# A diffusion-transformer block on one core: two modulation vectors computed ahead of V, a K tile split earlier, two LN2 chunks on another engine

## The chip, the cores and the metric

The kernel runs on one core of a Trainium2 chip. The metric is the device time of one execution in microseconds (us). The kernel before takes 244.02 us, the median of three runs (243.87 to 244.14). The profiled execution, whose trace is read below, took 243.82 us by the same clock; the trace itself spans 242.1 us from the first instruction to the last. All positions in this document are microseconds from the start of that span.

A core has five engines, each with a queue of its own: PE (TensorE, matmuls; PEld is its weight load), DVE (VectorE), ACT (ScalarE), POOL (GpSimd) and SP (SyncE, which issues most of the transfers here). [...]

## The reference

The block has two batch elements of 256 tokens, width D = 1152, two heads, and an MLP of width 4608. Everything that goes in and out is bfloat16. Cut to what matters:

```python
mod = (_silu(c) @ w_mod).reshape(B, 6, 1, D)
shift_a, scale_a, gate_a, shift_m, scale_m, gate_m = [mod[:, i] for i in range(6)]
h = _layernorm(x, axis=-1) * (1 + scale_a) + shift_a
qkv = (h @ wqkv).reshape(B, N, 3, H, Dh)
q, k, v = (qkv[:, :, 0].copy(), qkv[:, :, 1].copy(), qkv[:, :, 2].copy())
attn = _softmax(jnp.einsum('bqhd,bkhd->bhqk', q, k) * Dh ** (-0.5), axis=-1)
a = jnp.einsum('bhqk,bkhd->bqhd', attn, v).reshape(B, N, D) @ wo
x = x + gate_a * a
h2 = _layernorm(x, axis=-1) * (1 + scale_m) + shift_m
m = _gelu(h2 @ w_fc1) @ w_fc2
return x + gate_m * m
```

## The kernel before

Activations lie transposed, feature chunk by feature chunk: D is KD = 9 chunks of P = 128. The four token tiles (t = 0..3) are two for each batch element b. Weights go through a pool of five large buffers of 128 x 9 x 1152 elements, and a tile of the pool gets its place when it is first written.

**K and the shift.** K is computed from h without the shift: a constant added to all keys moves all scores of a row alike, and softmax drops it. Q and V need the shift. So K's tiles 0 to 5 run step by step as chunks arrive (`k_step`), its tiles 6, 7 and 8 run as whole panels, and inside the last panel the shift vector is computed, so that DVE and ACT can add it to h while PE finishes the panel.

```python
    for g, (k0, k1) in enumerate(KGROUPS):            # [(0, 2), (2, 4), (4, 6), (6, 9)]
        load_scale_group(g, nc.sync)
        for k in range(k0, k1):
            nc.sync.dma_start(w_k[:, k, 0:KM1 * P], wqkv_v[:, k, D:D + KM1 * P])       # KM1 = 6
    nc.sync.dma_start(w_k[:, :, KM1 * P:D], wqkv_v[:, :, D + KM1 * P:2 * D])
    # ... cut ...
    k_panel(6)
    k_evac(6)
    k_panel(7)
    k_evac(7)
    k_panel(8, 0, 5)                                  # chunks 0..4 of the last panel
    shift_a = vec_section(sT, w_shift_a, "shift_a")   # 36 narrow matmuls, then a DVE transpose
    k_panel(8, 5)                                     # chunks 5..8
    hT = act.tile([P, KD, T], BF16, name="hT")
    for k in range(KD):
        for b in range(B):
            dst, src = hT[:, k, b * N:(b + 1) * N], hT0[:, k, b * N:(b + 1) * N]
            if (k * B + b) % 3 < 2:
                nc.vector.tensor_scalar_add(dst, src, shift_a[:, k, b:b + 1])
            else:
                nc.scalar.activation(dst, src, ACT.Identity, bias=shift_a[:, k, b:b + 1])
        if k == 2:
            k_evac(8)
```

`vec_section` and `gate_natural` put the two rows of silu(c) on the array as a stationary operand of 32 columns and stream the weight past it, four column strips at a time. Q follows: six tiles together over the nine chunks (54 matmuls, line 511), then three tiles one by one (27, line 519), then the scores.

**The modulation vectors of the second half.** The gate of the attention branch (36 matmuls) goes through DRAM and comes back broadcast to all partitions. Two thirds of the MLP's scale are dot products on DVE against transposed weights (`scale_m_dots`); the last third (`scale_mN`) is 36 narrow matmuls. Both groups of matmuls stand after the second V group:

```python
    load_scale_mT(0)                                  # transposing load
    load_v(0)
    load_section("w_gate_a", S_GATE_A, w_gate_a)      # three pieces
    nc.sync.dma_start(w_scale_mN, wmod_v[:, :, S_SCALE_M * D + NDOT * P:(S_SCALE_M + 1) * D])
    load_v(1)
    load_scale_mT(CPP)
    load_v(2)
    # ... Q, the scores: cut ...
    for i, (pnl, t) in enumerate(v_order):            # 3 panels x 4 token tiles
        # softmax pieces and the transposes of the attention before the first three groups: cut
        v_group(pnl, t)                               # 9 matmuls 128x384, ACT copies the result
        if i == 1:
            gate_a = gate_natural(0, w_gate_a)
            scale_mN = vec_section(sT, w_scale_mN, "scale_mN", KD - NDOT)
        if i == 2:
            scale_m_dots(CPP, NDOT)
            # ... add one: cut ...
```

**LN2 and the start of FC1.** After the output projection (`wo_group(t, i)`), each token tile is normalized and transposed by a transfer into `hT`; `ln2_modulate` applies scale and shift in place. The nine chunks of batch 0 are modulated while PE still works on the output projection of tile 3; FC1 begins with batch 0 and takes the chunks in the order 0 to 8.

```python
    def ln2_modulate(b, ks=range(KD)):
        for k in ks:
            h = hT[:, k, b * N:(b + 1) * N]
            if b == 0 and k == KD - 1:
                nc.gpsimd.tensor_scalar(h, h, scale_m[:, k, b:b + 1], shift_m[:, k, b:b + 1], ...)
            elif b == 0 or k % 3 == 2:
                nc.scalar.activation(h, h, ACT.Identity, bias=shift_m[:, k, b:b + 1], scale=scale_m[:, k, b:b + 1])
            else:
                nc.vector.tensor_scalar(h, h, scale_m[:, k, b:b + 1], shift_m[:, k, b:b + 1], ...)
    # ...
    wo_group(3, 0)
    ln2_modulate(0, range(6))
    ln2_stats(2, 2)
    ln2_sqrt(2)
    ln2_modulate(0, range(6, KD))
    wo_group(3, 1)
    ln2_stats(3, 0)
    ln2_recip(2)
    ln2_normalize(2)
    ln2_transpose(2)
    wo_group(3, 2)
    wo_group(3, 3)
```

FC1 (432 matmuls, line 802) and FC2 (468, line 866) take the rest.

Of the kernel before, what the change touches and what calls it, by code (L numbers as in the profile page):

```python
# [19 lines left out]
def kernel(  # L20
# [11 lines left out]
    nc = tc.nc  # L32
    B, N, D = x.shape
# [3 lines left out]
    P = 128  # L37
# [3 lines left out]
    KD = D // P  # L41
# [17 lines left out]
    def acc_tile(shape, name, dt=FP32):  # L59
        return psum.tile(shape, dt, name=name, tag="acc", bufs=6)  # L60

    def aux_tile(shape, name, dt=FP32):
        return psum.tile(shape, dt, name=name, tag="aux", bufs=2)
# [5 lines left out]
    wqkv_v = wqkv.rearrange("(k p) n -> p k n", p=P)  # L69
# [7 lines left out]
    def wide_tile(name):  # L77
        return wide.tile([P, KD, D], BF16, name=name, tag="wide")
# [19 lines left out]

    KGROUPS = [(0, 2), (2, 4), (4, 6), (6, 9)]
    KM1 = 6  # L100
    w_scale_a = wide_tile("w_scale_a")
    w_k = wide_tile("w_k")

    def load_scale_group(g, eng):
        c0, c1 = KGROUPS[g][0] * P, KGROUPS[g][1] * P
        eng.dma_start(w_scale_a[:, :, c0:c1], wmod_v[:, :, S_SCALE_A * D + c0:S_SCALE_A * D + c1])

    for g, (k0, k1) in enumerate(KGROUPS):
        load_scale_group(g, nc.sync)
        for k in range(k0, k1):  # L110
            nc.sync.dma_start(w_k[:, k, 0:KM1 * P], wqkv_v[:, k, D:D + KM1 * P])
    nc.sync.dma_start(w_k[:, :, KM1 * P:D], wqkv_v[:, :, D + KM1 * P:2 * D])

    def load_section(name, s, w=None):
        w = wide_tile(name) if w is None else w
        for r in range(0, KD, 3):
            nc.sync.dma_start(w[:, r:r + 3, :], wmod_v[:, r:r + 3, s * D:(s + 1) * D])
        return w
# [9 lines left out]
    for r in range(0, KD, 3):  # L128
        nc.sync.dma_start(w_q[:, r:r + 3, 0:KM1 * P], wqkv_v[:, r:r + 3, 0:KM1 * P])
    nc.sync.dma_start(w_q[:, :, KM1 * P:D], wqkv_v[:, :, KM1 * P:D])  # L130
    w_scale_m = wide_tile("w_scale_m")
# [8 lines left out]
    def load_scale_mT(j):  # L140
        c0 = S_SCALE_M * D + j * P
        nc.sync.dma_start_transpose(w_scale_mT[:, j:j + CPP, :], w_mod[:, c0:c0 + PW])

    def load_o(n):
        nc.sync.dma_start(w_o[:, :, n * PW:(n + 1) * PW], wo_v[:, :, n * PW:(n + 1) * PW])
# [5 lines left out]
    def load_v(n):  # L151
        nc.sync.dma_start(w_v[:, :, n * PW:(n + 1) * PW], wqkv_v[:, :, 2 * D + n * PW:2 * D + (n + 1) * PW])
# [75 lines left out]
    def norm1(t, c0, c1, eng):  # L228
        if eng == "a":
            nc.scalar.activation(  # L230
                xns[t][:, c0:c1], x_sb[:, t, c0:c1], ACT.Identity,
                bias=nb1[:, t:t + 1], scale=rstd1[:, t:t + 1],
            )
        else:
            nc.vector.tensor_scalar(
                xns[t][:, c0:c1], x_sb[:, t, c0:c1], mv1[:, t, 0:1], rstd1[:, t:t + 1],
                op0=ALU.subtract, op1=ALU.mult,
            )
# [30 lines left out]
    def modulate(pt, i, k, t0, j0, w, eng):  # L269
        b = t0 // TPB  # L270
        dst, src, sc = hT0[:, k, t0 * P:t0 * P + w], pt[:, i, j0:j0 + w], scale_a[:, k, b:b + 1]
        if eng == "d":
            nc.vector.tensor_scalar_mul(dst, src, sc)
        else:
            nc.scalar.mul(dst, src, sc)
# [7 lines left out]

    def k_step(k, c0=0, c1=T, m0=0, m1=KM1):
        for m in range(m0, m1):
            if k == 0 and c0 == 0:
                pk[m] = acc_tile([P, T], "pk")
            nc.tensor.matmul(  # L288
                pk[m][:, c0:c1], w_k[:, k, m * P:(m + 1) * P], hT0[:, k, c0:c1],
                start=(k == 0 and c0 == 0), stop=(k == KD - 1), skip_group_check=True,  # L290
            )
# [19 lines left out]
    def k_evac(m):  # L311
        evac(kT[:, m, :], pk[m][:])

    def k_panel(m, ka=0, kb=KD):
        if ka == 0:
            pk[m] = acc_tile([P, T], "pk")
        for k in range(ka, kb):
            nc.tensor.matmul(  # L318
                pk[m][:], w_k[:, k, m * P:(m + 1) * P], hT0[:, k, :],
                start=(k == 0), stop=(k == KD - 1),  # L320
            )
# [70 lines left out]
    for k in range(2):  # L392
        modulate(pt_4, k, k, 3, 0, P, "d")
    k_step(3, 0, N, 3, KM1)
    norm1(1, CUT, D, "d")
# [31 lines left out]
    def vec_section(stat, w, name, nk=KD):  # L427
        pn = aux_tile([P, nk * 32], "pn")
        for k in range(KD):
            wk4 = w[:, k, :].rearrange("p (j q r) -> p q j r", q=4, r=32)  # L430
            for i in range(4):
                nc.tensor.matmul(  # L432
                    pn[32 * i:32 * i + SW, :].rearrange("p (j r) -> p j r", r=32),
                    stat[:, k, :], wk4[:, i, :, :],
                    start=(k == 0), stop=(k == KD - 1), tile_position=(0, 32 * i),
                )
        dst = act.tile([P, nk, 32], FP32, name=name)
        nc.vector.transpose(dst[:].rearrange("p k c -> p (k c)"), pn[:])
        return dst
# [2 lines left out]
    k_evac(6)  # L442
    k_panel(7)
    k_evac(7)
    k_panel(8, 0, 5)
    shift_a = vec_section(sT, w_shift_a, "shift_a")
    k_panel(8, 5)

    hT = act.tile([P, KD, T], BF16, name="hT")
    for k in range(KD):  # L450
        for b in range(B):
            dst, src = hT[:, k, b * N:(b + 1) * N], hT0[:, k, b * N:(b + 1) * N]
            if (k * B + b) % 3 < 2:
                nc.vector.tensor_scalar_add(dst, src, shift_a[:, k, b:b + 1])
            else:
                nc.scalar.activation(dst, src, ACT.Identity, bias=shift_a[:, k, b:b + 1])
        if k == 2:
            k_evac(8)
# [32 lines left out]
    for b in range(B):  # L491
        nc.sync.dma_start(s_b[b][:], s_dram[b:b + 1, :].partition_broadcast(P))
    load_scale_mT(0)
    load_v(0)
    load_section("w_gate_a", S_GATE_A, w_gate_a)
    nc.sync.dma_start(w_scale_mN, wmod_v[:, :, S_SCALE_M * D + NDOT * P:(S_SCALE_M + 1) * D])
    load_v(1)
    load_scale_mT(CPP)
    load_v(2)
# [81 lines left out]
    def v_group(pnl, t):  # L581
        pacc = acc_tile([P, PW], "pacc")
        for k in range(KD):
            nc.tensor.matmul(  # L584
                pacc[:], hT[:, k, t * P:(t + 1) * P], w_v[:, k, pnl * PW:(pnl + 1) * PW],
                start=(k == 0), stop=(k == KD - 1),
            )
        nc.scalar.copy(v_sb[:, t, pnl * PW:(pnl + 1) * PW], pacc[:])
# [3 lines left out]
    for i, (pnl, t) in enumerate(v_order):  # L592
        for j in ((0, 1), (2,), (3,))[i] if i < 3 else ():
            softmax(j // H, j % H)
            if j % H == H - 1:
                attn_transpose(j // H)
                for n in ((0,), (1, 2))[j // H]:
                    load_o(n)
        v_group(pnl, t)
        if i == 1:  # L600
            gate_a = gate_natural(0, w_gate_a)
            scale_mN = vec_section(sT, w_scale_mN, "scale_mN", KD - NDOT)
        if i == 2:
            scale_m_dots(CPP, NDOT)
            nc.vector.tensor_scalar_add(scale_m[:, 0:NDOT, :], scale_m[:, 0:NDOT, :], 1.0)
            nc.vector.tensor_scalar_add(scale_m[:, NDOT:KD, :], scale_mN[:, :, 0:B], 1.0)
# [52 lines left out]
    def ln2_recip(t):  # L659
        nc.vector.reciprocal(rstds[t][:], rstds[t][:])  # L660
        nbs[t] = small.tile([P, 1], FP32, name="nb", tag="nb")
        nc.vector.tensor_scalar(nbs[t][:], mv2[:, t, 0:1], rstds[t][:], -1.0, op0=ALU.mult, op1=ALU.mult)
# [16 lines left out]
# [4 lines that stand above are left out]
                nc.gpsimd.tensor_scalar(  # L683
                    h, h, scale_m[:, k, b:b + 1], shift_m[:, k, b:b + 1], op0=ALU.mult, op1=ALU.add,
                )
            elif b == 0 or k % 3 == 2:
                nc.scalar.activation(  # L687
                    h, h, ACT.Identity, bias=shift_m[:, k, b:b + 1], scale=scale_m[:, k, b:b + 1],
                )
            else:  # L690
                nc.vector.tensor_scalar(
                    h, h, scale_m[:, k, b:b + 1], shift_m[:, k, b:b + 1], op0=ALU.mult, op1=ALU.add,
                )
# [21 lines left out]
    def ln2_stats(t, i):  # L715
        c0, c1 = cuts[t][i:i + 2]
        nc.vector.bn_stats(stats2[t][:, i, :], x1[:, t, c0:c1])
# [33 lines left out]
    ln2_modulate(0, range(6))  # L751
    ln2_stats(2, 2)
    ln2_sqrt(2)
    ln2_modulate(0, range(6, KD))
    wo_group(3, 1)
    ln2_stats(3, 0)
    ln2_recip(2)
    ln2_normalize(2)
    ln2_transpose(2)
# [100 lines left out]
    for gi, (n, t, c0, cw) in enumerate(groups):  # L860
        b = t // TPB
# [59 lines left out]
```

## Time and profile before

| what | value |
|---|---|
| median of 3 runs | 244.02 us |
| span of the trace | 242.1 us |
| PE busy | 235.3 us, 1698 matmuls |
| DVE, ACT, POOL busy | 93.4, 69.5, 32.0 us |
| bytes moved | 54.48 MB, mean 225 GB/s |
| FC2, FC1 matmuls (lines 866, 802) | 70.5 us, 70.5 us |
| V matmuls (line 584) | 17.9 us |

The profile counts an engine busy from an instruction's start to its modelled end. Matmuls overlap, so a matmul listed with 379 ns can follow the one before it after 216 ns: the rate at which PE works is read from the starts, not from the durations. Four views matter here. The timeline of an engine lists its instructions in order of time, merged where they are alike, with start, length and count. The list of waits tells who waited for whom. The chain of waits goes back from the last instruction to what released it, step by step. The lines on transfers give the size and the time from issue to landing.

### The profile page before, as it was taken

The page shows a single profiled execution, that of the slowest core. Times are in us where ns is not written, and L with a number is a line of the kernel's source. Part 1 is how long each engine was busy: PE and PEld are TensorE (multiplying, and loading weights), DVE is VectorE, ACT ScalarE, POOL GpSimd, SP SyncE. Part 2 cuts the span into 40 slices and gives each one's busy share as a digit, 9 for nine tenths or more (in the row PEclk, how much of TensorE's full clock was granted, in tenths as well). Part 3 has the DMA queues.
Part 4 walks back from the last instruction along what each step waited for, and adds up shares of the span by engine and source line. Part 5 has one row for each costly group of instructions (what it writes and reads, how often), then busy time and mean ns, then how long its engine had stood idle before and what let it go on. Part 6 is the DMA issues. An engine that isn't in the chain of part 4 may idle for free.

```text
span 242.1 us, 4031 instructions
## 1 busy us (share of the span) xinstructions
PE 235.3 (97%) x1698; PEld 142.7 (59%) x1698; DVE 93.4 (39%) x209; ACT 69.5 (29%) x138; POOL 32.0 (13%) x48
## 2 busy tenths in 40 slices
PE   8799999999999999999999999999999999999994
PEld 2486444466656666888844444444566656665573
DVE  2872550675694676720000019999002000000001
ACT  6532250543735174782222233322000000000000
POOL 1000400000310616300000000000314111111111
PEclk9999999999999999999999999999999999999999
DMA  6999999999999999799999999996891000000000
GB/s 223 324 330 360 379 344 247 326 372 284 254 322 361 380 255 208 208 219 327 327 328 249 191 274 328 327 326 188 245 286 39 19 16 16 20 20 27 19 19 16
DMA packets 76989, 54.48 MB, mean 225 GB/s; under 512 B 26011, under 2 KB 72491, under 8 KB 76971
## 3 DMA queue, kind: packets, MB, share of 16 engines
q1 hardware_dynamic: 76240, 53.02, 77.7%
q0 software_dynamic: 704, 1.20, 1.6%
q8 instruction: 13, 0.21, 0.4%
q14 instruction: 5, 0.04, 0.0%
q10 hardware_dynamic: 27, 0.00, 0.0%
HBM read 46.90 MB, written 1.19 MB: 199 GB/s over the span
## 4 chain that ended last, share of the span: by engine, by line
PE 91%; DMA 3%; ACT 2%; DVE 2%; issue 0%; SPq 0%; DVEq 0%
PE pacc L866 29%; PE pacc L802 29%; PE pacc L584 7%; PE pacc L705 6%; PE pacc L511 5%; PE pk L288 4%; DMA w_scale_a<-in_w_mod_dram 3%; PE pacc L519 2%; PE pk L318 2%; ACT hT L687 2%; PE pa L619 1%; PE ps_s L539 1%; PE pn L432 1%; PE pm L248 1%; PE pt L266 1%; PE pg L467 1%
## 5 line engine op out<-in xcount | busy, mean ns | idle before, releaser
L802 PE MATMUL pacc<-hT,w_f 128*128 128x256 bf16 (+1 forms) x432 | 70.5, 326 | 0.2 <-ACT hT L687 0.2
L866 PE MATMUL pacc<-w_f,gT 128*128 128x384 bf16 (+2 forms) x468 | 70.5, 314 | 0.0
L866 PEld LDWEIGHTS <-gT 128*128 128x128 bf16 x468 | 44.4, 98 | 26.2
L802 PEld LDWEIGHTS <-w_f 128*128 128x128 bf16 x432 | 42.2, 98 | 28.0 <-issue 0.4
L485 DVE SCALAR_TENSOR_TENSOR late<-w_gate_mT,late 128x1152 bf16<-128x1152 bf16 x18 | 24.4, 1358 | 36.8 <-DMA w_gate_mT<-in_w_mod_dram 36.2
L872 DVE TENSOR_TENSOR tmp<-pacc,gate 128x384 f32<-128x384 f32 (+2 forms) x13 | 6.8, 527 | 62.5 <-PE pacc L866 50.5
L840 ACT ACTIVATE gT<-pacc 128x512 bf16<-128x512 f32 x24 | 14.3, 597 | 32.3 <-PE pacc L802 32.3
L485 DVE SCALAR_TENSOR_TENSOR s_spill<-w_scale_m,s_b 128x1152 bf16<-128x1152 bf16 x12 | 16.3, 1357 | 8.5 <-DMA w_scale_m<-in_w_mod_dram 8.2
L705 PE MATMUL pacc<-w_o,big 128*128 128x384 bf16 (+2 forms) x117 | 17.9, 314 | 0.0
L874 POOL TENSOR_TENSOR o_sb<-tmp,x 128x384 bf16<-128x384 f32 (+1 forms) x12 | 11.7, 974 | 47.4 <-DVE tmp L872 47.4
L584 PE MATMUL pacc<-w_v,hT 128*128 128x384 bf16 x108 | 17.9, 326 | 0.0
L705 PEld LDWEIGHTS <-big 128*128 128x128 bf16 x117 | 11.0, 98 | 6.8 <-ACT big L627 0.2
L584 PEld LDWEIGHTS <-hT 128*128 128x128 bf16 x108 | 10.4, 98 | 7.0 <-issue 0.2
L288 PE MATMUL pk<-big,w_k 128*128 128x128 bf16 (+2 forms) x102 | 13.3, 278 | 0.0
L711 POOL TENSOR_TENSOR x<-tmp,x_sb 128x384 f32<-128x384 f32 (+1 forms) x11 | 9.8, 891 | 17.4 <-DVE tmp L710 9.5
L511 PE MATMUL pacc<-hT,w_q 128*128 128x512 bf16 x54 | 11.8, 379 | 0.1
L327 POOL DMA_DIRECT2D gates_dram<-grow x4 | 2.1, 521 | 70.8 <-DVE grow L826 70.8
L818 ACT ACTIVATE gT<-pacc 128x512 bf16<-128x512 f32 x12 | 6.9, 597 | 10.4 <-PE pacc L802 10.4
L288 PEld LDWEIGHTS <-w_k 128*128 128x128 bf16 x102 | 7.8, 98 | 3.0
L511 PEld LDWEIGHTS <-w_q 128*128 128x128 bf16 x54 | 5.3, 98 | 6.7 <-issue 0.4
L710 DVE TENSOR_TENSOR tmp<-pacc,gate 128x384 f32<-128x384 f32 (+2 forms) x13 | 6.7, 522 | 5.4 <-PE pacc L705 5.2
L523 ACT ACTIVATE big<-pacc 128x512 bf16<-128x512 f32 x9 | 4.8, 608 | 11.5 <-PE pacc L511 8.8
(101 smaller groups left out, 160.9 us busy)
## 6 DMA issues: line engine op xcount, KB each, us to landing
w_f<-in_w_fc_dram SPq DMA_DIRECT2D x14, 864.0 KB, 11.0
w_f<-in_w_fc_dram SPq DMA_DIRECT2D x2, 2592.0 KB, 10.7
w_f<-in_w_fc_dram SPq DMA_DIRECT2D x2, 1728.0 KB, 13.8
w_shift_a<-in_w_mod_dram SPq DMA_DIRECT2D x3, 864.0 KB, 10.5
w_v<-in_wqkv_dram SPq DMA_DIRECT2D x3, 864.0 KB, 6.0
w_gate_a<-in_w_mod_dram SPq DMA_DIRECT2D x3, 864.0 KB, 9.2
w_o<-in_wo_dram SPq DMA_DIRECT2D x3, 864.0 KB, 6.2
w_shift_m<-in_w_mod_dram SPq DMA_DIRECT2D x3, 864.0 KB, 13.0
```

Source lines behind the costliest of these rows:

```text
L288: nc.tensor.matmul(pk[m][:, c0:c1], w_k[:, k, m * P:(m + 1) * P], hT0[:, k, c0:c1], start=(k == 0 and c0 == 0), stop=(k == KD - 1), skip_g ...
L485: nc.vector.scalar_tensor_tensor(spill, wT[:, j, :], 1.0, s_b[b], op0=ALU.mult, op1=ALU.mult, accum_out=dst(j, b),)
L511: nc.tensor.matmul(pq[m][:], w_q[:, k, m * P:(m + 1) * P], hT[:, k, :], start=(k == 0), stop=(k == KD - 1),)
L584: nc.tensor.matmul(pacc[:], hT[:, k, t * P:(t + 1) * P], w_v[:, k, pnl * PW:(pnl + 1) * PW], start=(k == 0), stop=(k == KD - 1),)
L705: nc.tensor.matmul(pacc[:], aT[:, k, t * P:(t + 1) * P], w_o[:, k, c0:c1], start=(k == ks[0]), stop=(k == ks[-1]),)
L711: (nc.vector if (t, i) in ((1, 2), (3, 3)) else nc.gpsimd).tensor_tensor(x1[:, t, c0:c1], tmp[:], x_sb[:, t, c0:c1], op=ALU.add)
L802: nc.tensor.matmul(dst, w_f1[m // KD][:, k, ml * P:(ml + 1) * P], hT[:, k, c0:c1], start=(k == 0), stop=(k == KD - 1),)
L818: nc.scalar.activation(gT[:, ms[0]:ms[-1] + 1, b * N:(b + 1) * N], pacc[:], ACT.Gelu_apprx_tanh)
L840: nc.scalar.activation(gT[:, m, :], pacc[:], ACT.Gelu_apprx_tanh)
L866: nc.tensor.matmul(pacc[:], gT[:, kk, t * P:(t + 1) * P], w_f2[j][:, r, c0 - n * PW:c0 - n * PW + cw], start=(kk == 0), stop=(kk == KF - 1),)
L872: nc.vector.tensor_tensor(tmp[:], pacc[:], gate_m[:, b, c0:c0 + cw], op=ALU.mult)
L874: (nc.vector if last else nc.gpsimd).tensor_tensor(o_sb[:], tmp[:], x1[:, t, c0:c0 + cw], op=ALU.add)
```

## The change

The change has three parts, all of them moves: the same values are computed with the same number of matmuls.

First, the attention gate and the last third of the MLP's scale are computed before the first V group instead of after the second, and their loads are issued ahead of the first V load. The first V group then begins with its matmuls after them.

Second, the last K panel is cut after 3 of its 9 chunks instead of after 5, so that the shift vector is computed sooner and six matmuls instead of four run while it is transposed and added. The adds are dealt differently: batch 0 and the odd chunks on DVE, the even chunks of batch 1 on ACT (13 and 5, before 12 and 6). The K weight's rows 6 to 8 are loaded whole, and the late load of columns 768 to 1151 shrinks to rows 0 to 5.

Third, two of the nine LN2 chunks of batch 0 (6 and 7) move from ACT to DVE, where they stand behind the first statistics of tile 3; the last chunk stays on POOL.

```diff
-            nc.sync.dma_start(w_k[:, k, 0:KM1 * P], wqkv_v[:, k, D:D + KM1 * P])
-    nc.sync.dma_start(w_k[:, :, KM1 * P:D], wqkv_v[:, :, D + KM1 * P:2 * D])
+            c1 = KM1 * P if k < KWHOLE else D          # KWHOLE = 6
+            nc.sync.dma_start(w_k[:, k, 0:c1], wqkv_v[:, k, D:D + c1])
+    nc.sync.dma_start(w_k[:, 0:KWHOLE, KM1 * P:D], wqkv_v[:, 0:KWHOLE, D + KM1 * P:2 * D])
...
-    k_panel(8, 0, 5)
+    k_panel(8, 0, 3)
     shift_a = vec_section(sT, w_shift_a, "shift_a")
-    k_panel(8, 5)
+    k_panel(8, 3)
...
-            if (k * B + b) % 3 < 2:
+            if b == 0 or k % 2:
                 nc.vector.tensor_scalar_add(dst, src, shift_a[:, k, b:b + 1])
...
     load_scale_mT(0)
-    load_v(0)
     load_section("w_gate_a", S_GATE_A, w_gate_a)
     nc.sync.dma_start(w_scale_mN, wmod_v[:, :, S_SCALE_M * D + NDOT * P:(S_SCALE_M + 1) * D])
+    load_v(0)
     load_v(1)
...
-        v_group(pnl, t)
-        if i == 1:
+        if i == 0:
             gate_a = gate_natural(0, w_gate_a)
             scale_mN = vec_section(sT, w_scale_mN, "scale_mN", KD - NDOT)
+        v_group(pnl, t)
...
-            elif b == 0 or k % 3 == 2:
+            elif k < 6 if b == 0 else k % 3 == 2:
                 nc.scalar.activation(
...
-    ln2_modulate(0, range(6, KD))
+    ln2_modulate(0, [KD - 1])
     wo_group(3, 1)
     ln2_stats(3, 0)
+    ln2_modulate(0, range(6, KD - 1))
     ln2_recip(2)
```

More of the change, by code (lines that the diff above doesn't have):

```diff
@@ L100 @@
     KM1 = 6
+    KWHOLE = 6
     w_scale_a = wide_tile("w_scale_a")
```

## The prediction

> **What bounds the kernel now.** I read the page's busy times first, then PE's waits, then PE's timeline at the three places that the change touches, and last the landings of the loads around V.
>
> ```profile
> PE 235.3 (97%) x1698; PEld 142.7 (59%) x1698; DVE 93.4 (39%) x209; ACT 69.5 (29%) x138; POOL 32.0 (13%) x48
> ...
> PE   8799999999999999999999999999999999999994
> ```
>
> PE is full from the second slice of 6 us to the last but one. The other engines and the transfers matter only where they make PE wait. The list of PE's waits has just one entry after the start-up:
>
> ```profile
> PE pacc L802 <- ACT hT L687: 0.2, 1, 0.2
> ```
>
> So no large gain is to be had: 2% would be 4.9 us, and the list has not 1 us of waits in the body. But the durations are modelled longer than the spacing, so a short gap can hide between a modelled end and the next start. I look for gaps in the starts.
>
> PE's timeline around the shift vector:
>
> ```profile
> 26.26 5.13 PE L318 MATMUL pk<-big,w_k 128*128 128x512 bf16 x23
> 31.32 1.29 PE L432 MATMUL pn<-w_shift_a,sT 128*32 128x288 bf16 x36
> 32.54 1.04 PE L318 MATMUL pk<-big,w_k 128*128 128x512 bf16 x4
> 33.72 2.53 PE L511 MATMUL pacc<-hT,w_q 128*128 128x512 bf16 x11
> ```
>
> A 128x512 matmul takes 0.216 us from start to start (27 of them take 5.83 us in line 519 of the chain of waits). Four from 32.54 use PE's time up to 33.41, but Q starts at 33.72: a gap of 0.31 us. VectorE and ScalarE at that time:
>
> ```profile
> 32.66 0.48 DVE L438 STREAM_TRANSPOSE shift_a<-pn 128x288 f32<-128x288 f32 x1 [3.56 <-PE pn L432]
> 33.18 0.87 DVE L454 TENSOR_SCALAR hT<-big,shift_a 128x256 bf16<-128x256 bf16 x4
> ```
>
> The first chunk needs two of these adds, both on DVE: the second starts 0.2 us after the first and takes 0.28, so the chunk is ready at 33.66, which is Q's start less a semaphore's delay.
>
> PE's timeline around V:
>
> ```profile
> 54.78 0.61 PE L548 MATMUL ps_s<-big 64*128 64x256 bf16 x8
> 55.33 3.10 PE L584 MATMUL pacc<-w_v,hT 128*128 128x384 bf16 x18
> 58.35 1.29 PE L467 MATMUL pg<-w_gate_a,sT 128*32 128x288 bf16 x36
> 59.47 0.56 PE L432 MATMUL pn<-w_scale_m,sT 128*32 128x96 bf16 x36
> 59.95 2.29 PE L584 MATMUL pacc<-w_v,hT 128*128 128x384 bf16 x13
> ```
>
> From 55.33 to 59.95 PE goes without a wait. The step is 0.163 us per V matmul (90 in 14.73 us in the chain of waits).
>
> PE's timeline at the start of FC1:
>
> ```profile
> 97.64 0.93 PE L802 MATMUL pacc<-hT,w_f 128*128 128x256 bf16 x7
> 98.75 2.45 PE L802 MATMUL pacc<-hT,w_f 128*128 128x256 bf16 x21 [0.18 <-ACT hT L687]
> ```
>
> Seven matmuls at 0.109 us (16 of 128x256 take 1.75 us in line 619 of the chain) reach to 98.40; the eighth, which needs chunk 7, starts at 98.75. The gap is 0.35 us and not the 0.18 counted. ACT's timeline tells why:
>
> ```profile
> 94.48 3.06 ACT L687 ACTIVATE hT<-hT,shift_m,scale_m 128x256 bf16<-128x256 bf16 x6 [3.60 <-DVE stats L717]
> 97.44 0.28 ACT L657 ACTIVATE rstd<-mv,eps_t 128x1 f32<-128x1 f32 x1
> 97.62 1.08 ACT L687 ACTIVATE hT<-hT,shift_m,scale_m 128x256 bf16<-128x256 bf16 x2
> ```
>
> Six chunks, a square root, then chunks 6 and 7, the last ready at 98.70.
>
> The loads around V, as SyncE issues them:
>
> ```profile
> 33.63 7.12 SPq L142 DMA_TRANSPOSE w_scale_m<-in_w_mod_dram  x1
> 40.80 0.58 SPq L152 DMA_DIRECT2D w_v<-in_wqkv_dram  x1
> 41.49 2.62 SPq L117 DMA_DIRECT2D w_gate_a<-in_w_mod_dram  x3
> 44.16 0.55 SPq L496 DMA_DIRECT2D w_scale_m<-in_w_mod_dram  x1
> ```
>
> Issue plus time to landing gives the arrivals. The transposing load took 10.7 us and lands at 44.3; V's first panel took 6.0, so 46.8; the gate's first and last piece 7.5 and 9.9, so 49.0 and (issued at 43.6) 53.5; the scale's third 12.1, so 56.3. They arrive in the order of issue, one behind the other: about 2.25 us per gate piece, 2.7 for the scale's third, 2.5 for V, all of 864 KB.
>
> **What the Trainium skill says.** TensorEngine Tiling (Array Packing), section Key Properties, says that a change of tiling mode drains the array. The trace agrees: the last K matmul before the narrow ones (128*32) is followed after 0.31 us instead of 0.216 (31.01 to 31.32), some 0.09 us per switch. ScalarE: Activation LUTs, section What ACT_TABLE_LOAD costs, gives 186 ns plus 93 for each pointer operand plus 0.833 ns an element, with an overlap of about 93 between neighbours. For 256 elements with scale and bias that is 585, stepping by 490; the trace has 583 to 600 and a step of 0.49, so moving two chunks frees ACT for 0.98 us. DMA: Bandwidth & Descriptors, section on queues, rings and completion order, says that each DMA engine consumes descriptors in ring order. That is why a load issued earlier pushes the later ones back; the staircase of arrivals above agrees.
>
> **The change part by part.** The shift. Two K matmuls of 0.216 us move behind the vector's, so the vector starts at 31.32 - 0.43 = 30.89. Its weight's last piece was issued at 19.3 and took 11.4 us, so it lands at 30.7, and only the last third of the 36 matmuls needs it, from about 31.7: no wait. The transpose is done at 33.14 - 0.43 = 32.71, and chunk 0 is added on DVE by 33.03 and on ACT (0.49 us for one, starting at 32.75) by 33.25. PE's six remaining K matmuls end at the same 33.41 as before, since the same work lies before it. Q starts there: -0.31 us. The accumulator of the last K tile, which Q's sixth matmul reuses, is copied by DVE after four adds, from 33.6 to 34.3; Q's sixth matmul comes at 33.41 + 5 x 0.216 = 34.5. No new wait. The wider K rows bring the last three row loads later by 0.25, 0.5 and 0.75 us (192 KB took 0.5 us here, 96 KB more each); the last was due at about 21, and its matmuls are the last six before 26.26. Nothing comes of it, nor of the smaller late load, whose panel starts at 26.26.
>
> The gate and the scale's third. They cost 58.35 to 59.95 = 1.60 us wherever they stand. Before V, they follow the scores' 64-row matmuls, where the mode changes anyway, so one switch (V to gate) drops out: 0.08 us. New are the times at which they and V are needed, 0.31 earlier than before: gate at 55.02, scale at 56.14, V at 56.6. The new arrivals are V's 2.5 us less for the three others, and V last: gate 46.6 to 51.1, scale 53.8, V 56.3 (56.5 if it takes 2.7). Gate and scale have over 2 us to spare, V has 0.1 to 0.3. I put 0.05 us for a short wait. ACT copies the gate about 3 us sooner, and it is broadcast sooner, but PE did not wait for it. The softmax keeps its place to within 0.1 us, since DVE and ACT pace it.
>
> LN2. ACT's six chunks end at about 97.2. DVE takes chunks 6 and 7 after the statistics, which ended at 97.38, now 97.1; with 0.35 us each, stepping by 0.25 (six of them were started between 106.3 and 107.6), they are ready at 97.45 and 97.7. FC1 starts at 97.3 and comes to chunk 6 at 97.98, to chunk 7 at 98.09. The gap closes: -0.35 us. Tile 2's reciprocal waits for the two, so DVE's work on tile 3 stays at its old place, while FC1 is 0.7 us ahead. Batch 1's modulation was done at 108.1, and FC1 gets there at 97.3 + 108 x 0.109 = 109.1: still 1 us to spare.
>
> The sum: -0.31 - 0.08 + 0.05 - 0.35 = -0.69, and PE is full behind it, so it reaches the end. 244.02 - 0.69 = 243.33 us.
>
> **The rivals.** First: V's load takes the place of the waits removed. For it speaks that its slack is only 0.1 to 0.3 us after 12 us of transfers in one chain; a chain 5% slower makes it 0.6 late, and PE waits 0.3 to 0.5 us. Against it: before, the same bytes landed at 56.3. The time would then be 243.7, in a bad case 244. Second: DVE becomes the bound at FC1. Chunk 6 stands behind statistics that wait for POOL's add, and if these don't move forward with PE, or if the transposing load of tile 1 (which lets ACT begin at 94.48) doesn't, the gap stays in part: 243.5 to 243.7. Slack for it is 0.4 us. Third: the gaps are not worth what the starts say, because Q's first nine chunks then run into the adds on ACT. Against it: an ACT add every 0.4 us feeds Q, which takes 6 x 0.216 = 1.3 us per chunk. If it were so, the first term would be lost: 243.65.
>
> **Range and chances.** The rivals all cost less than what is won, so the range runs from 242.9 (no V wait, and a little more at the switches) to 244.0 (two of the rivals). Faster or slower by 2% would need 4.9 us, and no place in the trace has it: 1% each.
>
> **What would show it.** Right: Q's first matmul at 33.4; the shift's at 30.9; gate at 55.0; V within 0.1 us of 56.6; FC1's first batch without a gap at chunk 7, and FC2 starting 0.7 us before its old place. Wrong: a wait of V's first matmul on w_v of over 0.3 us; a wait of FC1 on DVE at chunk 6; or a difference that arises past FC1, where nothing is changed.

## The result, and the profile after

The changed kernel takes 242.96 us, the median of six runs (242.57 to 243.56), beside 243.84 us for six runs of the kernel before: a ratio of 0.9964, with a 95% interval of 0.9949 to 0.9979. That is 0.88 us less, with an interval from 0.51 to 1.24. Predicted were 243.33 us and a ratio of 243.33 / 244.02 = 0.9972, which the interval holds. The profiled run took 242.85 us, its span is 241.1.

First, in the page of the changed kernel, the line of busy times and PE's row of the 40 slices:

```profile
PE 235.6 (98%) x1698; PEld 143.1 (59%) x1698; DVE 94.5 (39%) x212; ACT 68.1 (28%) x135; POOL 32.0 (13%) x48
...
PE   8899999999999999999999999999999999999994
```

PE does the same 1698 matmuls and is as full as before. Two chunks and one add have left ACT, and three have come to DVE: 138 to 135 and 209 to 212. The list of PE's waits (engine, tile and line, who was waited for, us in total, times, longest):

```profile
PE pm L250 <- DMA w_scale_a<-in_w_mod_dram: 0.5, 1, 0.5
PE pt L360 <- DVE xn L237: 0.2, 1, 0.2
```

These and one on a constant, ahead of all work, belong to the start-up, which the change doesn't touch. The wait of FC1 for ACT is gone, and none of V for its load has come. PE's timeline (start, us, instruction, count) around the shift vector:

```profile
30.67 1.29 PE L434 MATMUL pn<-w_shift_a,sT 128*32 128x288 bf16 x36
31.88 1.47 PE L320 MATMUL pk<-big,w_k 128*128 128x512 bf16 x6
33.19 3.19 PE L513 MATMUL pacc<-hT,w_q 128*128 128x512 bf16 x14
```

Six K matmuls at 0.216 us reach from 31.88 to 33.18, and Q starts at 33.19: the gap is closed. PE's timeline where V begins:

```profile
54.80 1.29 PE L469 MATMUL pg<-w_gate_a,sT 128*32 128x288 bf16 x36
55.91 0.56 PE L434 MATMUL pn<-w_scale_m,sT 128*32 128x96 bf16 x36
56.40 5.86 PE L586 MATMUL pacc<-w_v,hT 128*128 128x384 bf16 x35
```

V follows the scale in 0.49 us, as it did before (59.47 to 59.95), so it doesn't wait. SyncE's timeline has the loads in their new order:

```profile
33.28 6.87 SPq L144 DMA_TRANSPOSE w_scale_m<-in_w_mod_dram  x1
40.20 2.75 SPq L119 DMA_DIRECT2D w_gate_a<-in_w_mod_dram  x3
...
43.59 3.35 SPq L154 DMA_DIRECT2D w_v<-in_wqkv_dram  x1
```

They land at 43.69, 50.30 (the gate's last piece) and 55.72, and the scale's third between them at 53.01. V's panel is there 0.68 us ahead of its first matmul. At FC1, PE's timeline has one unbroken row, and ACT's and DVE's show the chunks:

```profile
97.02 4.20 PE L805 MATMUL pacc<-hT,w_f 128*128 128x256 bf16 x37
```

```profile
93.65 3.06 ACT L689 ACTIVATE hT<-hT,shift_m,scale_m 128x256 bf16<-128x256 bf16 x6 [3.40 <-DMA hT<-xn]
```

```profile
96.67 0.96 DVE L693 TENSOR_SCALAR hT<-hT,scale_m,shift_m 128x256 bf16<-128x256 bf16 x2
```

Chunks 6 and 7 are wanted after six and seven matmuls of 0.109 us, at 97.67 and 97.78. DVE ends them at 97.37 and 97.63, 0.1 us sooner than the 97.45 and 97.7 of the prediction. It is close, but nothing waits.

Where the time went, by comparing the starts of the two traces step by step. Each row is one stretch, in us:

| stretch | before | after | difference |
|---|---|---|---|
| start of the span to the first scale matmul | 9.13 | 8.91 | -0.22, not the change: nothing differs there, and it varies from trace to trace (8.39 to 9.22) |
| from there to Q | 24.58 | 24.28 | -0.30 |
| Q to V's third group, with gate and scale within | 26.24 | 26.15 | -0.09 |
| from there to FC1's first matmul | 37.69 | 37.68 | -0.01 |
| FC1's idle time ahead of chunk 7 | 0.35 | 0 | -0.35 |
| FC1's eighth matmul to the end | 143.30 | 143.30 | 0 |

The three terms of the change add up to -0.74; the span is 0.97 shorter because this run also reached its first matmuls 0.22 earlier. What was left to test: whether each part does this alone, whether its gain reaches the end, and how near the rivals were.

### The profile page after: what moved, and what is told of

It is laid out like the page before. It is cut to its first block, busy times and chain, and to the rows that moved or that the text cites. A ratio compares the mean times of both kernels' runs of the same rounds, so it can differ in the third digit from the quotient of the medians.

```text
span 241.1 us, 4034 instructions
## 1 busy us (share of the span) xinstructions
PE 235.6 (98%) x1698; PEld 143.1 (59%) x1698; DVE 94.5 (39%) x212; ACT 68.1 (28%) x135; POOL 32.0 (13%) x48
## 4 chain that ended last, share of the span: by engine, by line
PE 94%; DMA 3%; DVE 1%; ACT 0%; SPq 0%; issue 0%; DVEq 0%
PE pacc L869 29%; PE pacc L805 29%; PE pacc L707 7%; PE pacc L586 7%; PE pacc L513 5%; PE pk L290 4%; DMA w_scale_a<-in_w_mod_dram 3%; PE pk L320 2%; PE pacc L521 2%; PE pa L621 1%; PE ps_s L541 1%; PE pn L434 1%; PE pm L250 1%; PE pt L268 1%; PE pg L469 1%; SPq L85 0%
## 5 line engine op out<-in xcount | busy, mean ns | idle before, releaser
L173 PE MATMUL pwarm<-zeros 128*128 128x512 bf16 x21 | 7.6, 516 | 1.2 <-DVE eps_t L92 1.2
```

The source lines that it names most:

```text
L173: nc.tensor.matmul(dst[:], zeros[:, 0:P], zeros[:], start=True, stop=True)
```

## The experiments

The theory: each part closes its own gap, whatever the other parts do, and since PE is full behind it, the gain reaches the end. The rivals: V's load sets when PE goes on; the gap at FC1 is set by something other than ACT's queue, so that what PE gains ahead of FC1 is lost there; the shift's gain comes from the new deal of adds or the wider K rows, not from the split. Times are medians of runs that shared a chip with runs of the kernel before (median 243.6 to 243.65 us in each series, 242.7 to 245.0), and a ratio stands with its 95% interval. It is worked out from all runs of a series and is not the quotient of the two medians; the two differ by up to 0.0024.

### The parts alone

Only the split, at 3:

```diff
-    k_panel(8, 0, 5)
+    k_panel(8, 0, 3)
-    k_panel(8, 5)
+    k_panel(8, 3)
```

> The kernel before with the last K panel cut after 3 chunks instead of 5 and nothing else: the adds stay dealt as before (chunk 0 wholly on VectorE) and the K loads stay as before. My theory: the gap in front of Q (0.31 us between the end of the K work and Q's first matmul) closes, since even with both adds on VectorE chunk 0 is ready at about 33.23, before PE is done with K at 33.41; everything behind moves forward by 0.30 us, counted from the first scale matmul. The new deal of the adds and the wider K rows then do nothing. Rival: the new deal is needed; then part of the gap stays and the gain is 0.1 to 0.2 us.

Measured: 243.58 us, 0.9996 (0.9983 to 1.001). PE's timeline of this kernel:

```profile
31.67 1.47 PE L318 MATMUL pk<-big,w_k 128*128 128x512 bf16 x6
32.98 3.19 PE L511 MATMUL pacc<-hT,w_q 128*128 128x512 bf16 x14
...
96.91 1.06 PE L802 MATMUL pacc<-hT,w_f 128*128 128x256 bf16 x7
98.20 3.00 PE L802 MATMUL pacc<-hT,w_f 128*128 128x256 bf16 x26 [0.22 <-ACT hT L687]
```

Q comes 24.28 us after the first scale matmul (32.98 less 8.70), as in the changed kernel: the split alone closes the gap at Q, with the old deal of adds and the old K loads, so the third rival falls. But the gap at FC1 is 0.52 us here, where it was 0.35: seven matmuls from 96.91 are due to end at 97.67, and the eighth starts at 98.20. The time doesn't show 0.30 won; the interval runs from -0.41 to +0.24 us.

The same cut at 4, half the dose:

```diff
-    k_panel(8, 0, 5)
+    k_panel(8, 0, 4)
-    k_panel(8, 5)
+    k_panel(8, 4)
```

> The kernel before with the last K panel cut after 4 chunks: a half dose. Theory: the vector comes 0.216 us sooner and as much of the gap goes, 0.09 us of it stays; the gain is 0.21 us. Rival (the gap is a fixed cost of the switch between kinds of matmul and not a wait for chunk 0): no gain, or the same as with the cut at 3.

Measured: 243.82 us, 1.0 (0.9982 to 1.0019). Q comes at 24.36, so 0.22 of the 0.30 is won, as 0.216 us per matmul has it, and the gap can't be a fixed cost of the switch between kinds of matmul. Counted directly, the gap between the K work and Q is 0.30 us in all four traces with the cut at 5, 0.08 with the cut at 4 and 0 in all nine with the cut at 3. But FC1 in PE's timeline:

```profile
97.12 0.81 PE L802 MATMUL pacc<-hT,w_f 128*128 128x256 bf16 x5
98.16 0.27 PE L802 MATMUL pacc<-hT,w_f 128*128 128x256 bf16 x1 [0.22 <-ACT hT L687]
98.83 0.27 PE L802 MATMUL pacc<-hT,w_f 128*128 128x256 bf16 x1 [0.41 <-ACT hT L687]
99.33 1.91 PE L802 MATMUL pacc<-hT,w_f 128*128 128x256 bf16 x16 [0.22 <-ACT hT L687]
```

PE waits at chunks 4 to 7, 1.44 us in all. ACT began its six chunks at 95.05 and not at 94.48, because the transposing load of tile 1 landed at 94.95. The gain at Q is won and lost again, and more.

Only the move of gate and scale ahead of V, with their loads:

```diff
-    load_v(0)
     load_section("w_gate_a", S_GATE_A, w_gate_a)
     nc.sync.dma_start(w_scale_mN, ...)
+    load_v(0)
...
-        v_group(pnl, t)
-        if i == 1:
+        if i == 0:
             gate_a = gate_natural(0, w_gate_a)
             scale_mN = vec_section(sT, w_scale_mN, "scale_mN", KD - NDOT)
+        v_group(pnl, t)
```

> The kernel before with the gate's and the scale's matmuls and loads ahead of V and nothing else. Theory: one switch of the array's mode less, 0.08 to 0.09 us, and no wait of V for its load, since PE is here 0.3 us later than in the changed kernel. Rival one: V waits, and the gain is zero or negative. Rival two: gate and scale came too late for somebody before, and the gain is over 0.2 us.

Measured: 243.69 us, 1.0004 (0.9986 to 1.0021). V's third group comes 0.09 us earlier, counted from the first scale matmul (50.73 for 50.82). The panel landed at 56.30, V wanted it at 56.90: no wait for the load. The gap at FC1 is 0.14. The time can't resolve 0.09.

Only the two LN2 chunks:

```diff
-            elif b == 0 or k % 3 == 2:
+            elif k < 6 if b == 0 else k % 3 == 2:
...
-    ln2_modulate(0, range(6, KD))
+    ln2_modulate(0, [KD - 1])
     wo_group(3, 1)
     ln2_stats(3, 0)
+    ln2_modulate(0, range(6, KD - 1))
```

> The kernel before with LN2 chunks 6 and 7 of batch 0 on VectorE and nothing else. Theory: the 0.35 us in front of FC1's matmul for chunk 7 go away and nothing comes back later, so -0.35 us. Rival: VectorE is late with chunk 6, or tile 2's later reciprocal makes FC1 wait at batch 1, and less than 0.2 us is won.

Measured: 243.18 us, 0.9976 (0.9966 to 0.9985), so 0.37 to 0.83 us less: the one part whose time alone leaves zero outside. FC1 in PE's timeline is unbroken:

```profile
97.37 3.87 PE L803 MATMUL pacc<-hT,w_f 128*128 128x256 bf16 x34
```

It is worth 0.58 us by the ratio and 0.42 between the medians, where the gap in the trace of before gave 0.35, and its 20 runs lie closer together (242.88 to 243.68) than those of before. Both fit a gap that isn't a constant: with ACT's old queue it was 0.14, 0.35, 0.52 and 1.44 us in four traces, and in this one it is 0.

### How near the rivals are

V's second panel loaded ahead of the first, in the changed kernel, so that V must wait:

```diff
-    load_v(0)
-    load_v(1)
+    load_v(1)
+    load_v(0)
```

> The changed kernel with V's second panel loaded ahead of its first, so that the first lands one load (2.7 us) later. It measures how near the changed kernel is to a wait. V's first panel landed at 55.7 and was wanted at 56.4 there; now it lands at about 58.4. Theory: PE waits 2.0 us at V's first matmul and all of it reaches the end: +2.0 us over the changed kernel. Rival: the queue behind (softmax, copies, later loads) takes a part of it up, since VectorE and ScalarE pace the softmax: +1 us or less.

Measured: 245.4 us in four runs, 1.0086 (1.0061 to 1.0111), +2.1 us against before by the ratio (1.8 between the medians) and, between the medians, +2.4 against the changed kernel of the same series (243.0 below). PE's timeline:

```profile
59.14 3.08 PE L586 MATMUL pacc<-w_v,hT 128*128 128x384 bf16 x18 [2.36 <-DMA w_v<-in_wqkv_dram]
```

The wait of 2.36 us comes out at the end in full: from V's third group on this trace needs 181.75 us, the changed kernel's 181.74. V's load is thus a real bound, with 0.68 us to spare in the first trace of the changed kernel and only 0.07 in its second (landed at 55.91, wanted at 55.98). Panel 1 landed at 56.47, and V went on 2.67 us behind it, about the time of one more transfer of 864 KB. This agrees with what the prediction took from the Trainium skill (DMA: Bandwidth & Descriptors, section Queues, rings and completion order), that each DMA engine takes descriptors in ring order. The same section does not promise that loads complete in the order of issue; that they did is what the landings here show.

The changed kernel with the old order of loads:

```diff
     load_scale_mT(0)
+    load_v(0)
     load_section("w_gate_a", S_GATE_A, w_gate_a)
     nc.sync.dma_start(w_scale_mN, ...)
-    load_v(0)
```

> The changed kernel with the loads of gate, scale and V in the order of the kernel before (V's first panel first) and the matmuls in the new order. The scale's third then lands last, at about 55.7, and is wanted at 55.9. Theory: no wait, or under 0.1 us; the time is that of the changed kernel within 0.1 us, and moving the loads was not needed. Rival: the scale's third is late and PE waits 0.3 us or more.

Measured: 243.07 us, 0.9981 (0.9972 to 0.9989). PE's timeline where the scale is computed:

```profile
56.06 0.57 PE L434 MATMUL pn<-w_scale_m,sT 128*32 128x96 bf16 x36 [0.23 <-DMA w_scale_m<-in_w_mod_dram]
```

In the changed kernel the scale follows the gate's start after 1.11 us (54.80 to 55.91). Here the gate starts at 54.54, so the scale was due at 55.65 and came 0.41 late: its weight landed at 56.01. My expectation was wrong. In this trace the loss reaches the end, since from V's third group on it needs 181.75 us as well. Yet the time is that of the changed kernel within the intervals. How many of the 20 executions have this wait is not known, so a gain from the new order of loads is not shown in the time.

The changed kernel with only chunk 7 on DVE:

```diff
-            elif k < 6 if b == 0 else k % 3 == 2:
+            elif k < 7 if b == 0 else k % 3 == 2:
...
-    ln2_modulate(0, [KD - 1])
+    ln2_modulate(0, [6, KD - 1])
...
-    ln2_modulate(0, range(6, KD - 1))
+    ln2_modulate(0, range(7, KD - 1))
```

> The changed kernel with only chunk 7 on VectorE; chunk 6 stays on ScalarE behind the square root. It is then ready at about 97.1 + 0.6 - 0.1, and FC1 comes to it at about 97.4. Theory: ScalarE's chunk 6 is ready before FC1 wants it or within 0.1 us of it, so one chunk moved does nearly all of the 0.35 us: the time is that of the changed kernel within 0.1 us. Rival: chunk 6 was late as well, and 0.15 us or more come back.

Measured: 243.56 us, 0.9994 (0.9975 to 1.0013). FC1 in PE's timeline:

```profile
98.33 0.27 PE L805 MATMUL pacc<-hT,w_f 128*128 128x256 bf16 x1 [0.22 <-ACT hT L689]
99.00 2.23 PE L805 MATMUL pacc<-hT,w_f 128*128 128x256 bf16 x19 [0.41 <-ACT hT L689]
```

PE waits for chunks 4, 5 and 6 on ACT, 1.02 us in all, because the transposing load of tile 1 landed at 95.11, 4.53 us after its issue; in the two traces of the changed kernel it took 3.27 and 3.29. That is the second rival: the load sets it, and not the count of chunks alone. So the trace doesn't settle whether one chunk is enough. With a load as late, two chunks leave a wait too (0.49 us in the first kernel with the gate's piece brought forward, below). Had the load taken 3.27 us, chunk 6 would by the same spacing have been ready at about 97.7, and FC1 wanted it at 97.98 (an estimate). The intervals of the two times overlap.

The changed kernel itself in the same series, for a second trace:

> The changed kernel once more, for its time against the kernel before and for a second trace. Theory: 0.75 us of the difference is in the three places (0.30, 0.09, 0.36), and the 0.22 us by which the first trace was ahead already at the first scale matmul is the arrival of the first loads, which differs from run to run; so the place of the first scale matmul moves by some tenths between traces, while the three steps stay within 0.03 us. Rival: the start is really faster, and stays 0.2 us ahead.

Measured: 243.0 us in 19 runs (242.59 to 244.62), 0.9982 (0.9968 to 0.9995). This trace began 0.5 us earlier than the first of the changed kernel (first scale matmul at 8.39 for 8.91) and yet ends at the same place, with a span of 241.0. The start does vary, but the three steps did not stay within 0.03 us: Q comes 24.38 us after the first scale matmul and not 24.28, since 0.10 us went to short waits between 11.7 and 13.2. More was lost later, as PE's timeline shows:

```profile
79.26 6.02 PE L707 MATMUL pacc<-w_o,big 128*128 128x384 bf16 x36 [0.23 <-DMA w_o<-in_wo_dram]
```

The third panel of w_o landed at 79.22, and PE stood 0.39 us in front of it (the 0.23 is again counted from a modelled end). PE came early, the load did not, and these two losses took up the 0.5 us.

### Can the loads be brought forward?

If the stream of loads sets the pace up to FC1, an earlier load should help. V's first panel issued before the two loads of s_b and the first transposing load, in the kernel before, and then with the split at 3 as well:

```diff
+    load_v(0)
     for b in range(B):
         nc.sync.dma_start(s_b[b][:], s_dram[b:b + 1, :].partition_broadcast(P))
     load_scale_mT(0)
-    load_v(0)
```

> The kernel before with V's first panel issued ahead of the two small loads of silu(c) and of the first transposing load, where SyncE stood idle for 5 us; nothing else. The traces so far say: FC1's chunk 7 is ready 4.3 us after the last transposing load of batch 0 (hT) lands, and that load lands either 3.3 us after its own issue (PE paces it) or 3.4 us after the second FC1 load (the stream of loads paces it). Theory: with the stream 1 to 2.5 us ahead, hT is paced by its issue, so the stall in front of chunks 6 and 7 is 0.1 to 0.35 us in every trace; the time falls by 0.2 to 0.5 us against the kernel before. Rival: the stream does not get ahead, because the transposing load or the softmax paces it, and the time stays.

> The same early load of V with the K panel cut after 3 chunks. Theory: with hT paced by PE the 0.30 us of the earlier cut, which did not show in the time of split3 alone, now reach the end: 0.2 to 0.3 us below the kernel with the early V load. Rival: they are again lost at FC1 (same time, stall 0.3 us longer).

Measured: 244.64 us, 1.0035 (1.0013 to 1.0056), and 244.6 us, 1.0036 (1.0019 to 1.0054). Both are slower, and the theory was wrong. SyncE's timeline of the first:

```profile
28.13 4.57 SPq L152 DMA_DIRECT2D w_v<-in_wqkv_dram  x1
32.97 4.26 SPq L493 DMA_DIRECT2D s_b<-s_dram  x2
37.27 8.11 SPq L142 DMA_TRANSPOSE w_scale_m<-in_w_mod_dram  x1
```

The issue of that load held SyncE for 4.57 us and the next two for 4.26, so the transposing load was issued at 37.27 instead of 33.63 and landed at 47.96 instead of 44.32. The gate's pieces behind it came 2 us late, and PE waited 1.59 us for w_o's third panel and 1.43 in FC1. With the split it was 0.18 and 1.43.

The gate's first piece brought forward in the same way, in the changed kernel; and the same with w_q loaded in three pieces of whole rows:

```diff
+    nc.sync.dma_start(w_gate_a[:, 0:3, :], wmod_v[:, 0:3, S_GATE_A * D:(S_GATE_A + 1) * D])
     for b in range(B):
         nc.sync.dma_start(s_b[b][:], s_dram[b:b + 1, :].partition_broadcast(P))
...
     # second kernel only: w_q by rows, in place of its pieces of 768 columns and the rest
+    for r in (0, 3, 6):
+        nc.sync.dma_start(w_q[:, r:r + 3, :], wqkv_v[:, r:r + 3, 0:D])
```

> The changed kernel with the first piece of the gate's weight issued ahead of the two small loads and the first transposing load. Theory: the stream of loads gets up to 2.3 us ahead, the third panel of the output weight no longer comes just in time (0.39 us of wait in the second trace of the changed kernel), and the time falls by 0.1 to 0.4 us below the changed kernel. Rival: the first transposing load comes 2 us later, the dot products on VectorE end after the scores, the softmax is late, and the time rises.

> The same, and Q's weight loaded in three pieces of whole rows (2304 bytes each) instead of four pieces with rows of 1536 and 768 bytes. Whole rows took 2.26 us per 864 KB in the trace, rows of 768 bytes 2.7. Theory: Q's load ends some 0.7 us sooner and takes the later first transposing load back; as fast as the kernel with the gate's piece early, or up to 0.2 us faster. Rival: the first piece, now half as big again, lands after Q wants it (33.2), and PE waits 0.3 us or more.

Measured: 245.73 us, 1.0061 (1.0042 to 1.0081), and 242.91 us, 0.9969 (0.9957 to 0.9982). The first repeats the failure: the transposing load landed at 46.6, and PE waited 0.81 us for V's panel, 1.96 for w_o's panels and 0.49 in FC1. That last wait comes although two chunks are on DVE: tile 1's load took 4.57 us, and ACT's own chunks 4 and 5 were late. PE's timeline:

```profile
99.97 0.82 PE L807 MATMUL pacc<-hT,w_f 128*128 128x256 bf16 x5
101.01 2.23 PE L807 MATMUL pacc<-hT,w_f 128*128 128x256 bf16 x19 [0.22 <-ACT hT L691]
```

In the second kernel none of these waits is left (w_o's third panel landed at 77.84), and its time equals that of the changed kernel; no version here beats it clearly.

What the traces say together, in us. The second column is the time of tile 1's transposing load from issue to landing:

| kernel | tile 1's load | tile 1 landed | ACT's first chunk | FC1 starts | idle in FC1 | w_o wait | span |
|---|---|---|---|---|---|---|---|
| before | 3.47 | 94.37 | 94.48 | 97.64 | 0.35 | 0 | 242.1 |
| moved gate and scale alone | 3.27 | 94.04 | 94.14 | 97.51 | 0.14 | 0 | 241.7 |
| split at 3 alone | 3.65 | 93.82 | 93.92 | 96.91 | 0.52 | 0 | 241.5 |
| split at 4 alone | 4.57 | 94.95 | 95.05 | 97.12 | 1.44 | 0.10 | 242.6 |
| one chunk on DVE | 4.53 | 95.11 | 95.22 | 97.33 | 1.02 | 0.09 | 242.4 |
| two chunks alone | 3.48 | 94.10 | 94.20 | 97.37 | 0 | 0 | 241.4 |
| changed | 3.27 | 93.54 | 93.65 | 97.02 | 0 | 0 | 241.1 |
| changed, second trace | 3.29 | 93.53 | 93.64 | 96.99 | 0 | 0.39 | 241.0 |
| changed, old loads | 3.62 | 94.04 | 94.15 | 97.17 | 0 | 0 | 241.2 |
| changed, gate's piece early | 4.57 | 97.80 | 97.90 | 99.97 | 0.49 | 1.96 | 244.5 |

With ACT's old queue, chunk 7 is ready 4.33 us after tile 1 has landed, in the first four traces (94.37 to 98.70, 94.04 to 98.37, 93.82 to 98.15, 94.95 to 99.28). FC1 wants it 0.76 us after its start, and it starts 6.74 to 6.75 us after the issue of tile 1's load in every trace: PE's progress sets both. So with the old queue the idle time is what that load takes less 3.13 us. In the ten traces where it took 3.33 us or more, it landed 3.35 to 3.43 us after the second FC1 panel, which speaks for the stream of loads setting it there. In the other four it took 3.27 to 3.29. PE's gain ahead of FC1 is lost where the stream doesn't move forward with it.

## Why the prediction was right, and where it was off

**The shift, -0.31.** Right: -0.30, with the split alone as the cause. The places named for it (33.4 for Q, 56.6 for V) were met 0.2 us early, because the trace reached its first matmuls 0.22 earlier. That the wider K rows and the new deal give nothing was right too; the kernel without them reaches Q at the same 24.28.

**The gate and the scale, -0.08.** Right: -0.09 in the changed kernel and alone.

**V's wait, +0.05.** No wait was measured, but the slack was small, as forecast. The term was worked out from landings of 56.3 against a need at 56.6. In the first trace V landed at 55.72 and was wanted at 56.40, because the stream of loads itself came some 0.6 us earlier (first transposing load at 43.69 for 44.32), which I had held fixed; in the second the slack was 0.07. That the slack is consumed one for one once it is gone, v1_first showed with 2.36 us.

**LN2, -0.35.** The mechanism was right, and the trace has exactly that gap less. But the size was taken from one trace as if it were a constant, and that it came out to the hundredth is luck. In the changed trace tile 1's load took 3.27 us, so even ACT's old queue would have left an idle time of only about 0.14 (an estimate from the trace of the gate and scale moved alone, whose load also took 3.27); the other 0.21 came from the faster load. The gap is 0.14 to 1.44 us in the traces with ACT's old queue, and the part alone was worth 0.58 by the ratio (0.37 to 0.83), 0.42 between the medians. This is the term of the sum that was mis-sized.

Two small slips change nothing: PE's row is full from the third slice on, not the second, which is a 7; and with FC1's start at 97.3, six and seven steps of 0.109 us lead to 97.95 and 98.06, not 97.98 and 98.09.

**"PE is full behind it, so it reaches the end."** This holds from FC1's eighth matmul on: the two traces need the same 143.30 us from there. It holds less well ahead of FC1. The second rival said that the gap stays if "the transposing load of tile 1" doesn't move forward. It did not in the kernels with the split at 4 and with one chunk, where the second FC1 panel landed at 91.53 and 91.70 (before: 90.97) and tile 1 3.4 us behind it; the 0.22 us won at Q went into FC1's gap. In the second trace of the changed kernel 0.39 us went into w_o's wait. With two chunks on DVE the first of these two leaks is closed as long as tile 1's load takes no more than 3.62 us, and at 4.57 it is 0.49 instead of 1.44. That the LN2 part thereby lets the gains of the other two arrive is likely, but not shown.

**The other rivals.** V's load as the bound: its mechanism shown, but not its case. Q running into ACT's adds: no; Q goes on without a break.

**What stays open.** That the split and the move of the gate shorten the whole time by 0.30 and 0.09 was read in traces only. The intervals of their times alone contain both zero and that gain. Nor is the changed kernel clearly faster than its LN2 part alone: against before, the ratio is 0.9964 (0.9949 to 0.9979) and 0.9982 (0.9968 to 0.9995) in two series for the whole change, and 0.9976 (0.9966 to 0.9985) for the part. The two measurements of the whole, 0.88 us less (0.51 to 1.24) and 0.44 less (0.12 to 0.78), have 0.51 to 0.78 in common, where the sum of the prediction, 0.69, lies; with intervals so wide that is no proof of its three terms.

## What to carry to other kernels

A gap in one trace between two streams that run abreast, here PE and the loads, is a sample and not a constant: look at what sets each end of it, and expect it to move when either is touched. A short gain ahead of such a meeting point counts only with slack on the other side; making that slack (two chunks to an idle engine) was worth 0.42 to 0.58 us where the gap seen was 0.35. And a load put ahead in a full queue delays what stands behind it, so look first at who is waiting there.

## What the runs showed that I had not expected

An issue can hold SyncE for long: 4.57 us for V's panel when it was issued at 28.13, with none of Q's four loads landed yet (33.0 to 38.9), where 0.58 us sufficed in the kernel before, after they had landed. That the full stream is the reason is likely, but no run varied it alone.

The transposing load of tile 0 landed 0.90 to 0.95 us after the second FC1 panel in three traces (91.66 against 90.76 in the changed kernel) and 2.45 to 2.48 in ten (93.44 against 90.97 before); in the fourteenth, with V's panels exchanged, it was issued too late to compare. In those ten, tile 1 landed 3.35 to 3.43 us after the panel. In the late case the view of transfers from 86 to 96 us of the kernel before has a stretch of silence:

```profile
DMA  9999999999999900000993000069999942699999
```

Slices are 0.25 us. The quiet from 89.5 to 90.75 (22 GB/s and less) is there in the changed kernel too, some 0.25 to 0.5 us sooner (50 GB/s and less), but the second one, from 91.5 to 92.5, is a single slice there:

```profile
DMA  9999999999999431119960999999525799999999
```

What fills or empties this time isn't settled. A single 16 KB packet of instructions near 89 us took about 2.5 us in the late trace of before and 1 us in the early one of the changed kernel, but the kernel with the two chunks alone was late with a packet of 1 us, so the packet doesn't explain it.
